# A load moved from SyncE's queue to GpSimd's, a memset moved to VectorE, and another written-out order of 976 steps

## The chip, the cores and the metric

The kernel runs on one core of one Trainium2 chip. The metric is the time of one execution on the device in microseconds, the median of several runs. The engines are called by the profile's short names: PE is TensorE, PEld its weight loads, DVE VectorE, ACT ScalarE, POOL GpSimd and SP SyncE.

## The reference, cut to what matters

Attention without a softmax, through a feature map of degree two, and then a dense layer of width 2048 with a rational activation:

```python
def phi(x):                                       # S1, S2: [8, 32]
    a = np.einsum('rd,bhsd->bhsr', S1, x)
    b = np.einsum('rd,bhsd->bhsr', S2, x)
    return np.einsum('bhsi,bhsj->bhsij', a, b).reshape(*x.shape[:-1], 64)
q_p, k_p = phi(q), phi(k)                         # q, k, v: [4, 4, 1088, 32]
kv, z = np.einsum('bhsf,bhsd->bhfd', k_p, v), np.sum(k_p, axis=2)
x = einsum(q_p, kv) / (einsum(q_p, z) + 1e-06)    # -> [4352, 128]
h = x @ w_in                                      # [128, 2048]
P = a[0] + a[1] * h + a[2] * h**2 + a[3] * h**3
Q = 1.0 + np.abs(b[0]) * np.abs(h) + np.abs(b[1]) * h**2
out = (P / (Q + 1e-06)) @ w_out                   # [2048, 128]
```

All inputs and the output are float32.

## The kernel before

The program is one list of 976 steps. A step is a few instructions of one engine, with the steps that it comes after and the buffers that it uses. `step` (L88) gives the step its place in the program from the tuple `PLACE` (L165), by the number of the step in the order in which the code makes it, and `run` (L99) emits all steps sorted by place. Every engine works through its own instructions in that order. The numbers for cost, rate, slack and `early` that the calls of `step` and `dma` carry are read by nothing in this file; they are the inputs of a planner that wrote `PLACE`. `ON_ACT` (L215) lists the steps that go to ScalarE where either ScalarE or VectorE could do them. `FILLS` (L219) says ahead of which places TensorE gets matmuls on the zero block `idle` that compute nothing; one more is put ahead of all.

Instructions that are not steps are emitted where the code stands, ahead of all steps: GpSimd's memsets of `idle` (L317), of `ones`, the identity, the masks and the constant parts of `v_sb`, `kT` and `kvz` (L318 to L336).

The stages, as far as they are touched:

- S1 and S2 (8x32 each) are loaded into the two halves of `s_raw` by SyncE, k of batch 0 ("k0", 544 KB) by ScalarE's queue, q of batch 0 in two parts and v of batch 0 in two halves by SyncE (L290 to L296), then w_in in two halves, w_out in two halves and k of batch 1 (L303 to L314). A load that finds its DMA semaphore taken waits on the queue for the earlier load that holds it.
- `mk_rep` (L351, DVE) repeats `s_raw` into `s_rep`, `mk_st` (L348, PE) transposes it, `mk_s12` and `mk_sab` (L354, L359, DVE) multiply it with masks into `S12`, the weights of the keys' sketches, and `SAB`, those of the queries'.
- `keys` (L407): VectorE transposes k in blocks of 32 into `kT` (L415, L417), TensorE makes the sketches (L435), ScalarE copies one half of them (L440), VectorE multiplies the halves to features (L443), TensorE adds up features times values (L454), and ScalarE keeps the result in `kvz` (L471).
- `queries` (L487): a transpose of q (L496), sketches (L518 or L546), features (L530, L533, or, through a round trip to DRAM of two puts and three gets, L554), the product with `kvz` (L586), the quotient (L595 to L602), a transpose on TensorE (L608) and the copy into `xT` by ScalarE (L615).
- `w_part` (L385): ten pieces of w_out go to bfloat16, five versions of two halves, `y` 0 to 4; versions 0, 1, 3 and 4 are multiplied by a coefficient (L391, L395), version 2 is a plain copy (L393, L397). Each piece goes to ScalarE or VectorE by `ON_ACT`.
- `unit` (L672): some blocks of 128 hidden channels by up to 512 tokens, 3072 columns in most units, 256 to 2048 in the first and the last ones. TensorE computes h (L688), ScalarE evacuates it (L692), VectorE takes the absolute value (L703), `any_w` (L706: L708 on VectorE, L710 on ScalarE) and L713 form Q, ScalarE inverts it by logarithm and exponential (L716, L719), VectorE forms the powers times the inverse (L728 to L749), and TensorE multiplies by w_out (L784). When a tile of tokens is done VectorE transposes it (L796) and it is written out in pieces (L808).

Of the kernel before, what the change touches and what calls it, by code (L numbers as in the profile page):

```python
# [20 lines left out]
def kernel(  # L21
# [103 lines left out]
    def d_four(n, ptr):  # L125
# [88 lines left out]
    )  # L214
    ON_ACT = (  # L215
        24, 26, 28, 29, 31, 32, 328, 351, 379, 454, 478, 502, 535, 612, 636, 669, 688, 693, 744, 878, 889,
        914, 932, 946, 951, 953, 960,
    )
    FILLS = {5: 15, 14: 4, 66: 5, 70: 1}  # L219
    NW = 5 if '4' in MODES else 3  # L220


    TC = 512
# [32 lines left out]
    def flat(x, b):  # L256
        return x[b].rearrange("h (g j) d -> (h g) (j d)", g=32)
# [605 lines left out]
```

## Time and profile before

| | |
|---|---|
| median of 3 runs | 266.96 us (266.92 to 267.07) |
| the profiled execution | 267.34 us |
| its span, first to last instruction | 265.5 us |
| mean granted TensorE clock | 0.996 |
| DVE busy / ACT busy / PE busy | 252.7 / 248.4 / 257.2 us |
| last instruction of VectorE | 261.75 us, 0.45 long |

The span is what the rows of the profile add up to; the profiled execution is 1.84 us longer than its span. A busy PE is not PE at its peak: matmuls are pipelined, and their ends are modelled. Where an instruction starts before the one ahead of it on its engine has ended, the two overlap in the pipeline, so that distances from start to start say more than durations.

### The profile page before, as it was taken

What the parts mean: (1) busy time and instruction counts of PE and PEld (TensorE: products, weight loads), DVE (VectorE), ACT (ScalarE), POOL (GpSimd) and SP (SyncE); (2) the same over time, 40 slices, a digit from 0 to 9 for tenths busy, and PEclk for the clock granted to TensorE, in tenths of its full rate; (3) what the DMA queues carried; (4) which work ended last, traced back from release to release, by engine and by line L of the source; (5) the groups of instructions that cost most, each with busy time, mean ns of one, the idle gap of its engine ahead of it and who ended that gap; (6) DMA issues with size and microseconds to landing.
All of it is one profiled execution on the core that took longest, in us unless ns stands there. A gap on an engine that the chain in (4) does not pass through costs nothing.

```text
span 265.5 us, 4239 instructions
## 1 busy us (share of the span) xinstructions
PE 257.2 (97%) x1663; PEld 140.4 (53%) x1663; DVE 252.7 (95%) x293; ACT 248.4 (94%) x209; POOL 2.7 (1%) x25
## 2 busy tenths in 40 slices
PE   7999999999999999999999999999999999999994
PEld 5767645644544464344445555444444476565682
DVE  3989899999999999999999999999999999999994
ACT  2499999999999999999999999999999999999991
POOL 4000000000000000000000000000000000000000
PEclk9999999999999999999999999999999999999998
DMA  7948344620556503035001522200002002010032
GB/s 202 331 151 223 121 127 118 159 61 0 145 131 168 164 2 108 13 79 131 28 6 44 150 65 46 41 0 0 0 10 32 0 0 40 4 29 11 0 52 40
DMA packets 29063, 20.13 MB, mean 76 GB/s; under 512 B 19316, under 2 KB 24948, under 8 KB 29044
## 3 DMA queue, kind: packets, MB, share of 16 engines
q1 hardware_dynamic: 28352, 19.24, 28.8%
q10 hardware_dynamic: 692, 0.62, 0.8%
q8 instruction: 13, 0.21, 0.4%
q14 instruction: 6, 0.05, 0.1%
HBM read 16.65 MB, written 3.21 MB: 75 GB/s over the span
## 4 chain that ended last, share of the span: by engine, by line
PE 35%; ACT 29%; DVE 21%; issue 8%; DMA 4%; SPq 1%; DVEq 0%; ACTq 0%
PE h_ps L688 21%; ACT t L692 7%; ACT ln L716 7%; ACT t L719 7%; PE out_ps L784 6%; ACT t L725 5%; DVE t L713 4%; DVE t L728 4%; DVE t L731 3%; DMA kq<-in_q_dram 3%; DVE t L749 2%; PE att_ps L586 2%; DVE t L703 2%; PE att_ps L546 2%; DVE t L708 2%
## 5 line engine op out<-in xcount | busy, mean ns | idle before, releaser
L688 PE MATMUL h_ps<-xT,w_in_sb 128*128 128x512 f32 (+1 forms) x320 | 128.0, 535 | 0.8 <-ACT xT L615 0.6
L784 PE MATMUL out_ps<-t,w_out 128*128 128x512 bf16 (+1 forms) x498 | 101.7, 346 | 0.6 <-DVE t L728 0.5
L688 PEld LDWEIGHTS h_ps<-xT,w_in_sb 128*128 128x128 f32 x320 | 58.6, 190 | 45.2 <-issue 33.8
L784 PEld LDWEIGHTS <-w_out 128*128 128x128 bf16 x498 | 47.4, 98 | 51.9 <-issue 21.1
L692 ACT CAST t<-h_ps 128x1024 bf16<-128x1024 f32 (+1 forms) x69 | 68.5, 1025 | 0.9 <-PE h_ps L688 0.9
L716 ACT ACTIVATE ln<-t 128x3072 f32<-128x3072 bf16 (+4 forms) x29 | 64.7, 2230 | 0.3 <-DVE t L713 0.2
L719 ACT ACTIVATE t<-ln 128x3072 bf16<-128x3072 f32 (+4 forms) x29 | 64.7, 2232 | 0.1
L713 DVE TENSOR_TENSOR t<-t,t 128x3072 bf16<-128x3072 bf16 (+4 forms) x29 | 40.4, 1392 | 0.6 <-ACT t L710 0.6
L728 DVE TENSOR_TENSOR t<-t,t 128x3072 bf16<-128x3072 bf16 (+4 forms) x29 | 40.4, 1394 | 0.0
L731 DVE TENSOR_TENSOR t<-t,t 128x3072 bf16<-128x3072 bf16 (+3 forms) x23 | 32.6, 1423 | 0.1
L725 ACT ACTIVATE t<-t,a_sb 128x3072 bf16<-128x3072 bf16 (+2 forms) x12 | 32.0, 2665 | 0.0
L703 DVE TENSOR_SCALAR t<-t 128x3072 uint16<-128x3072 uint16 (+4 forms) x29 | 22.5, 776 | 0.3 <-ACT t L692 0.2
L734 DVE TENSOR_TENSOR t<-t,t 128x3072 bf16<-128x3072 bf16 (+1 forms) x13 | 21.6, 1660 | 0.0
L708 DVE TENSOR_SCALAR t<-t,b_abs 128x3072 bf16<-128x3072 bf16 (+2 forms) x22 | 21.5, 975 | 0.1
L586 PEld LDWEIGHTS att_ps<-kvz,a_all 128*64 128x64 f32 x288 | 9.6, 137 | 6.8 <-issue 2.2
L586 PE MATMUL att_ps<-kvz,a_all 128*64 128x66 f32 x288 | 11.5, 226 | 0.6 <-DVE a_all L530 0.4
L749 DVE TENSOR_TENSOR t<-t,t 128x1024 bf16<-128x1024 bf16 (+3 forms) x10 | 11.2, 1124 | 0.1
L710 ACT ACTIVATE t<-t,b_abs 128x1024 bf16<-128x1024 bf16 (+4 forms) x7 | 11.3, 1611 | 0.0
L554 DVE TENSOR_TENSOR a_all<-a_all,b_all 128x768 f32<-128x768 f32 (+2 forms) x11 | 9.6, 869 | 0.0
L443 DVE TENSOR_TENSOR k_p<-att_ps,b_sk 128x768 f32<-128x768 f32 x9 | 8.4, 949 | 0.8 <-ACT b_sk L440 0.6
L454 PEld LDWEIGHTS att_ps<-v_sb,k_p 128*64 128x64 f32 x216 | 6.7, 138 | 2.3 <-issue 1.3
L746 DVE TENSOR_TENSOR t<-t,t 128x3072 bf16<-128x3072 bf16 (+3 forms) x6 | 7.7, 1276 | 0.0
(74 smaller groups left out, 143.8 us busy)
## 6 DMA issues: line engine op xcount, KB each, us to landing
a_all<-sk_d SPq DMA_DIRECT2D x6, 384.0 KB, 3.9
b_all<-sk_d SPq DMA_DIRECT2D x12, 192.0 KB
kq<-in_k_dram SPq DMA_DIRECT2D x3, 544.0 KB, 7.3
kq<-in_q_dram SPq DMA_DIRECT2D x3, 544.0 KB
a_all<-sk_d SPq DMA_DIRECT2D x4, 320.0 KB
b_all<-sk_d SPq DMA_DIRECT2D x8, 160.0 KB
v_sb<-in_v_dram SPq DMA_DIRECT2D x4, 288.0 KB, 4.9
v_sb<-in_v_dram SPq DMA_DIRECT2D x4, 256.0 KB, 4.3
```

The source lines that it names most:

```text
L586: nc.tensor.matmul(nd.t[x:x + 64, o:o + 2 * KW], lhsT=(av(c)[:, o0 + x:o0 + x + 64] if how == "direct" else q_p.t[:, c * n + o0 + x:c * n ...
L688: nc.tensor.matmul(h.t[:, cols[x] - cols[x0]:cols[x + 1] - cols[x0]], lhsT=w_in_sb[:, f * 128:(f + 1) * 128], rhs=xT[:, xpos(t0):xpos(t0) ...
L692: nc.scalar.copy(out=hh.t[:, cols[x0]:cols[x1]], in_=h.t[:, 0:cols[x1] - cols[x0]])
L703: nc.vector.tensor_scalar(out=u.t[:, :n].bitcast(U16), in0=hh.t[:, :n].bitcast(U16), scalar1=0x7FFF, scalar2=None, op0=AX.bitwise_and)
L708: nc.vector.tensor_scalar(out=w.t[:, :n], in0=u.t[:, :n], scalar1=ab1, scalar2=ab0, op0=AX.mult, op1=AX.add)
L713: nc.vector.tensor_mul(out=y.t[:, :n], in0=w.t[:, :n], in1=u.t[:, :n])
L716: nc.scalar.activation(out=ln.t[:, :n], in_=y.t[:, :n], func=ACT.Ln, bias=1.0 + 1e-6)
L719: nc.scalar.activation(out=r.t[:, :n], in_=ln.t[:, :n], func=ACT.Exp, scale=-1.0)
L725: nc.scalar.activation(out=p.t[:, :n], in_=hh.t[:, :n], func=ACT.Identity, scale=a3, bias=a2)
L728: nc.vector.tensor_mul(out=s.t[:, :n], in0=hh.t[:, :n], in1=r.t[:, :n])
L731: nc.vector.tensor_mul(out=(hh if mode == 3 else p).t[:, :n], in0=hh.t[:, :n], in1=s.t[:, :n])
L784: nc.tensor.matmul(o[0].t[:, :bl[x][1]], lhsT=w_sb[y_][:, bl[x][2], :], rhs=src.t[:, cols[x]:cols[x + 1]], start=(o[1] == 1), stop=(o[1] = ...
```

## The change

S2's load is no longer a step of SyncE. It is issued by GpSimd where the code stands, ahead of GpSimd's constants, and step 1 is kept as an empty step of GpSimd that later steps come after. `idle` is set to zero by VectorE instead of GpSimd. The numbers given to the planner are others, and with them `PLACE`, `ON_ACT` and `FILLS`. No other step computes anything else or in another form.

Sorted from the two tuples, the first steps of some queues are, by the names of the code:

```
SP before:  S1, S2, q0 first part, v0 low, v0 high, q0 rest, w_out 2nd half, w_out 1st half, w_in 1st half, k1, put, w_in 2nd half
SP after:   S1, q0 first part, v0 low, v0 high, w_out 2nd half, q0 rest, k1, w_out 1st half, w_in 1st half, put, put, w_in 2nd half
DVE before: mk_rep, k0 transposes, mk_s12, q0 transpose, mk_sab, mk_sab, features, k0 transposes, features
DVE after:  mk_rep, mk_s12, k0 transposes, mk_sab, mk_sab, q0 transpose, k0 transposes, features, features
```

`ON_ACT`: of w_out's pieces ScalarE had versions 0, 1 and 4 of the first half, 2 of both and 3 of the second; it has now versions 1, 3 and 4 of the first half and 0, 1 and 3 of the second. Step 946, an `any_w` of 768 columns in the last but one unit, goes from ScalarE to VectorE. The fills are 18 instead of 26.

```diff
--- before.py
+++ after.py
@@ -163,60 +163,60 @@
     PERS = (6,)
     N_T = 16
     PLACE = (
-        0, 3, 1, 19, 6, 7, 8, 2, 18, 16, 9, 58, 55, 12, 10, 4, 5, 13, 24, 25, 49, 21, 23, 22, 83, 97, 84,
...
+        0, 1, 2, 18, 3, 4, 8, 11, 12, 27, 14, 73, 24, 25, 9, 5, 6, 7, 15, 16, 52, 13, 22, 21, 105, 47, 82,
...
     )
     ON_ACT = (
-        24, 26, 28, 29, 31, 32, 328, 351, 379, 454, 478, 502, 535, 612, 636, 669, 688, 693, 744, 878, 889,
-        914, 932, 946, 951, 953, 960,
+        25, 26, 27, 30, 31, 32, 328, 351, 379, 454, 478, 502, 535, 612, 636, 669, 688, 693, 744, 878, 889,
+        914, 932, 951, 953, 960,
     )
-    FILLS = {5: 15, 14: 4, 66: 5, 70: 1}
+    FILLS = {6: 12, 13: 3, 71: 1, 80: 1}
     NW = 5 if '4' in MODES else 3
 
 
@@ -288,12 +288,17 @@
         return dma(s_raw[i * R:(i + 1) * R], s_in, rank, 0.001, eng=eng, cost=0.4, slack=S_SLACK[i], behind=behind)
 
     s_l = [load_s(0, -206, SP)]
-    s_l.append(load_s(1, -205.9, SP, behind=s_l[0]))
+    nc.gpsimd.dma_start(out=s_raw[R:2 * R], in_=S2)
+
+    def go():
+        pass
+
+    s_l.append(step(POOL, 0.65, go, -205.9, land=0.003, early=0.75, slack=0.4))
     FIRST = 256
-    k0_l = load_k(0, k0, -207, slack=0.0, rate=304, eng=ACTE)
+    k0_l = load_k(0, k0, -207, slack=0.15, rate=420, eng=ACTE)
     table = step(ACTE, 1.3, lambda: nc.scalar.preload_act_table_set("natural_log_exp_and_others"), -205, behind=k0_l[0])
-    q0_a = dma(lambda: q0.t[:, 0:FIRST], flat(q, 0)[:, 0:FIRST], -203.8, 0.131, (), [q0], rate=250, slack=0.1, behind=s_l[1])
-    v0_l = load_v(0, v0, -203.7, slack=0.25, rates=(180, 200), behind=q0_a)
+    q0_a = dma(lambda: q0.t[:, 0:FIRST], flat(q, 0)[:, 0:FIRST], -203.8, 0.131, (), [q0], rate=350, slack=0.2, behind=s_l[0])
+    v0_l = load_v(0, v0, -203.7, slack=0.4, rates=(340, 205), behind=q0_a)
     ab_in = []
     for c, w, x in ((4, 2, moe_b), (0, 4, moe_a)):
         ab_in.append(dma(ab_row[:, c:c + w], bass.AP(tensor=x.tensor, offset=x.offset, ap=[[w, 1], [1, w]]), -203.6, 0.001,
@@ -302,19 +307,19 @@
 
     def load_w(x, rank):
         c = x * 1024
-        w_l[x] = dma(w_in_sb[:, c:c + 1024], moe_w_in[:, c:c + 1024], rank, 0.524, early=LATER, rate=300, slack=0.4, behind=v0_l[1])
+        w_l[x] = dma(w_in_sb[:, c:c + 1024], moe_w_in[:, c:c + 1024], rank, 0.524, early=LATER, rate=430, slack=0.4, behind=v0_l[1])
 
     load_w(0, -196)
-    q0_b = dma(lambda: q0.t[:, FIRST:S], flat(q, 0)[:, FIRST:S], Q0B_RANK, 0.426, (), [q0], rate=200, slack=0.3, behind=q0_a)
+    q0_b = dma(lambda: q0.t[:, FIRST:S], flat(q, 0)[:, FIRST:S], Q0B_RANK, 0.426, (), [q0], rate=330, slack=0.4, behind=q0_a)
     load_w(1, W1_RANK)
     k1 = Buf("kq")
-    k1_l = load_k(1, k1, K1L_RANK, early=LATER, slack=0.2, behind=v0_l[1], rate=350)
+    k1_l = load_k(1, k1, K1L_RANK, early=LATER, slack=1.3, behind=v0_l[1], rate=390)
     wo_l = [dma(lambda f0=f0: w_raw.t.rearrange("p (f d) -> p f d", d=d_model)[:, f0:f0 + nf // 2],
                 moe_w_out.rearrange("(fo fi) d -> fi fo d", fi=128)[:, f0:f0 + nf // 2], WO_RANK, 0.525, (), [w_raw],
-                early=LATER, rate=310, slack=0.4, behind=v0_l[1]) for f0 in (0, nf // 2)]
+                early=LATER, rate=318, slack=0.4, behind=v0_l[1]) for f0 in (0, nf // 2)]
 
     idle = consts.tile([128, 256], BF, name="idle")
-    nc.gpsimd.memset(idle, 0.0)
+    nc.vector.memset(idle, 0.0)
     nc.gpsimd.memset(ones, 1.0)
 
     def fill(x):
@@ -367,7 +372,7 @@
             nc.gpsimd.tensor_copy(out=S21[:, :, :, :, hp], in_=S12[:, 2 * hp:2 * hp + 2].rearrange("p h s r -> p s h r"))
 
     st = step(DVE, 0.15, mk_rep, -210, after=s_l)
-    st = step(PE, 0.11, mk_st, -202, after=[st], uses=[s_ps], early=2.7)
+    st = step(PE, 0.11, mk_st, -202, after=[st], uses=[s_ps], early=2.0)
     s12 = [step(DVE, 0.15, mk_s12, -200, after=[st], uses=[s_ps])]
     sab = [step(DVE, 0.2, lambda i=i: mk_sab(i), -201.5 + 0.1 * i, after=[st], uses=[s_ps]) for i in range(2)]
     s21 = step(POOL, 0.4, mk_s21, -196, after=s12)
@@ -560,16 +565,16 @@
             put = [dma(lambda j=j: bass.AP(tensor=d.t.tensor, offset=d.t.offset + j * n2,
                                            ap=[[2 * QN, half], [n, 2], [1, n2]]),
                        lambda j=j: c.t[j * 2 * half:(j + 1) * 2 * half, :n2],
-                       rank, n2 * 256e-6, [st], [c, d], rate=260, slack=GAP) for j in range(2)]
+                       rank, n2 * 256e-6, [st], [c, d], rate=200, slack=GAP) for j in range(2)]
             puts[-1] = put[-1]
             get = [dma(lambda: a.t[:, :2 * n],
                        lambda: bass.AP(tensor=d.t.tensor, offset=d.t.offset, ap=[[2 * QN, 2 * R], [0, R], [1, 2 * n]]),
-                       rank, n * 1.024e-3, put, [d, a], rate=230, cost=0.57, slack=GET_SLACK)]
+                       rank, n * 1.024e-3, put, [d, a], rate=230, cost=0.57, slack=GET_SLACK - 0.2)]
             for h2 in range(2):
                 get.append(dma(lambda h2=h2: bb.t[h2 * 64:(h2 + 1) * 64, :2 * n],
                                lambda h2=h2: bass.AP(tensor=d.t.tensor, offset=d.t.offset + (2 + h2) * R * 2 * QN,
                                                      ap=[[0, R], [2 * QN, R], [1, 2 * n]]),
-                               rank, n * 0.512e-3, put, [d, bb], rate=85, cost=0.6, slack=GET_SLACK, behind=get[-1]))
+                               rank, n * 0.512e-3, put, [d, bb], rate=95, cost=0.6, slack=GET_SLACK, behind=get[-1]))
 
             ft = step(DVE, d_one(2 * n), features, rank, after=get, uses=[a, bb])
 
```

(The tuple `PLACE` is cut to its first line.)

94 rows, old and new, of the table PLACE are left out of this document.

## The prediction

> **What bounds the kernel now.** I read the page's busy times first, then the busy times in windows of 10 us, then the waits, then the first microseconds of the timeline and of the chain of waits.
>
> ```profile
> PE 257.2 (97%) x1663; PEld 140.4 (53%) x1663; DVE 252.7 (95%) x293; ACT 248.4 (94%) x209; POOL 2.7 (1%) x25
> ```
>
> ```profile
> 0.00:10.00 10.00, 8.08 (x109) 6.10 (x110) 5.43 (x16) 2.90 (x10) 2.74 (x25) 1.00 0.87 237
> 10.00:20.00 10.00, 9.44 (x111) 6.95 (x107) 8.63 (x24) 8.11 (x14) 0.00 (x0) 1.00 0.70 221
> 20.00:30.00 10.00, 10.00 (x153) 7.83 (x151) 9.45 (x18) 9.43 (x14) 0.00 (x0) 1.00 0.73 209
> 30.00:40.00 10.00, 9.44 (x51) 4.16 (x48) 9.45 (x17) 9.19 (x14) 0.00 (x0) 1.00 0.38 103
> 60.00:70.00 10.00, 10.00 (x52) 4.90 (x52) 10.00 (x12) 10.00 (x9) 0.00 (x0) 1.00 0.06 13
> 250.00:260.00 10.00, 10.00 (x93) 8.91 (x92) 9.86 (x16) 9.78 (x12) 0.00 (x0) 1.00 0.23 34
> ```
>
> The columns of a window are its length and then the busy time of PE, PEld, DVE, ACT and POOL. VectorE (DVE) works 252.7 us, starts at 4.50 and ends at 262.2, so it stands idle for only 257.7 - 252.7 = 5.0 us on the way, half of that before 35 us. ScalarE is almost as full from 15 us on. The time is therefore VectorE's start, plus its work, plus its stalls, plus 3.3 us of the last transposed block's way out. A change of order can only move these terms.
>
> ```profile
> DVE s_rep L352 <- DMA s_raw<-in_S_dram: 4.5, 1, 4.5
> DVE qT L496 <- DMA kq<-in_q_dram: 0.7, 1, 0.7
> ACT kvz L471 <- PE out_ps L454: 1.7, 1, 1.7
> ```
>
> VectorE starts when S1 and S2 lie in `s_raw`, and has one stall on a load, 0.73 us at 29.8. The first row is what the change aims at:
>
> ```profile
> 0.73 0.74 SPq L268 DMA_DIRECT2D s_raw<-in_S_dram  x2
> 0.74 0.38 ACTq L268 DMA_DIRECT2D kq<-in_k_dram  x1
> ...
> 1.10 0.40 PE L321 MATMUL out_ps<-idle 128*128 128x256 bf16 x1 [1.10 <-POOL idle L317]
> ...
> 4.50 0.21 DVE L352 COPY s_rep<-s_raw 16x128 f32<-16x128 f32 x1 [4.50 <-DMA s_raw<-in_S_dram]
> 4.65 0.75 DVE L415 STREAM_TRANSPOSE kT<-kq 128x256 f32<-128x256 f32 x2
> 4.87 0.20 PE L349 MATMUL att_ps<-ident,s_rep 16*128 16x16 f32 x1 [0.44 <-DVE s_rep L352]
> 5.33 0.17 DVE L355 TENSOR_TENSOR S<-att_ps,mask 128x64 f32<-128x64 f32 x1
> 5.44 0.41 DVE L496 STREAM_TRANSPOSE qT<-kq 128x256 f32<-128x256 f32 x1
> 5.79 0.44 DVE L362 TENSOR_TENSOR SAB<-att_ps,mask 128x128 f32<-128x128 f32 x2
> 6.17 0.42 DVE L443 TENSOR_TENSOR k_p<-h_ps,b_sk 128x256 f32<-128x256 f32 x1
> ```
>
> The semaphore records of the same trace say that S1 landed at 2.17, k0 at 4.36 and S2 at 4.41. S1 and S2 are equal (1 KB), S2 was issued 0.46 us later. The packet records tell why it came 2.24 us later: S1's eight packets ran from 1.68 to 1.85, just ahead of k0's first (1.75); each of S2's eight began 6 ns after k0's last packet on its DMA engine (3.28 to 3.64). An engine that has begun k0's eight rows finishes them first.
>
> **The change, part by part.** The sum is made against the profiled execution (267.34 us, span 265.5), which is 0.38 above the median of the runs; differences are put on the median.
>
> *S2 by POOL.* SP loses one issue, so q0's first part and both halves of v0 are issued 0.33 to 0.46 earlier (1.19 to 1.52, and on). That is worth nothing: after k0 the DMA engines are busy without a gap (share 0.88 to 1.17 in every half microsecond to 7 us), q0's packets follow k0's in any case, and v0 (7.6 for its second half) is no earlier for an earlier issue. On POOL the constants lose the zero block (0.25, spacing 0.73 to 0.98) and stand behind the new issue instead. POOL ends at 3.2 now and the identity at 1.7; nothing asks for them before the transpose of `s_rep`. Even 1.3 us more is hidden there. If the cover is gone, mk_st waits on the identity.
>
> The order of VectorE's first steps, sorted from the new places, is s_rep, S12, k0's two transposes, SAB twice, q0's transpose; now it is s_rep, k0's transposes, S12, q0's transpose, SAB twice. So k0's transposes now queue behind S12, which waits for a TensorE transpose of s_rep. With S2 landing at L: s_rep at L + 0.09 (4.41 to 4.50), mk_st 0.37 later (4.50 to 4.87) and 0.20 long, S12 some 0.10 after that, k0's transposes 0.11 behind it (5.33 to 5.44): L + 0.87. The rest to the first features is 0.68 (4.65 to 5.33) + 0.35 + 0.38 = 1.41, so features begin at L + 2.28 against 6.17: **a shift of L - 3.89**. It can't be better than k0's landing allows: 4.36 + 0.09 + 1.41 = 5.86, a gain of 0.31, reached with L at 3.58 or less.
>
> What is L? No row shows a data DMA issued by POOL. Bounds: the lower end is S1's way, 0.73 to 2.17, if POOL's packets reach the engines by 1.7; the upper is 0.73, an issue as long as SP's longest here (0.75) and S2's present way of 3.22, so 4.7, and behind q0's eight packets on an engine (46 ns each, 0.37) 5.1. Between them a threshold decides: S2's own packets at SP's 0.94 us from issue to first packet would come at 1.68, but k0's engines start at 1.75. 0.1 us of slowness puts S2 behind k0. I take the missed case, with k0's last engine done at 3.97 and a receipt of 0.5 to 0.8 as S2 has now: **L = 4.5, shift +0.6**; ends -0.3 and +1.2.
>
> The Trainium skill ("DMA: Bandwidth & Descriptors", Specifications) gives a first byte of about 1 us for GpSimd's software path and 0.6 for SP's; by it S2's packets would come 0.4 after S1's, at an estimated 2.1, behind k0, and the sum would stay as it is. The same page ("Why a DMA increments its semaphore by 16 and not by 1") says that on this path all 16 engines post the completion whatever the shape; no run here shows that yet, and it would tie S2 to k0's slowest engine instead of eight of them.
>
> *Zero block by VectorE, fills 26 to 18.* VectorE is idle until 4.5, so the memset is free; TensorE's fills may begin up to 0.2 earlier. Thirteen fills at 0.209 (3.14 us for 15) end about 3.7 and hide nothing. Price zero, unless the clock warms later for it: the granted clock was full in the first window it was recorded, and the fills at 5.00 ran in 0.15 each. Bounds 0 and +0.5; I take 0.
>
> *The new order.* The load of q for batch 1, issued at 23.20 behind two puts, goes ahead of one of them; at most the stall of 0.73 goes. ScalarE gets two pieces of w_out (1.16 each, L391) into its idle 1.70 before kvz; it needs w_out's half by 9.3, and that half is now loaded before q0's rest. VectorE's stalls from 10 to 35 us are 2.5 in sum. I take **-0.5**; ends -1.2 and +0.6 (a new stall of the size of those that are there). The price of moving k1 and w_out ahead of w_in: w_in's first half landed at 13.47 and one more load of 1.5 us stands ahead of it now, 15.0, while the first hidden matmul runs at 15.85. 0.85 covers it.
>
> *Who does what.* Step 946, any_w on 768 columns, goes from ScalarE (1.02, L710) to VectorE: 0.48 from L708's 0.54 for 1024 and 0.81 for 2048. It lies in the last 12 us, where VectorE is 9.86 of 10 busy, so it counts in full. Of w_out's ten pieces VectorE swaps two scaled ones (0.74 each) for plain copies, which no row of VectorE shows; ScalarE's are 1.05 against 1.16, so I take -0.1 each, ends 0 and -0.3. Net **+0.3**; ends +0.1 and +0.5.
>
> Sum: +0.6 - 0.5 + 0.3 = +0.4, so 266.96 + 0.4 = **267.4**.
>
> **Rivals.** *S2 slips in ahead of k0* (L under 3.6): -0.3 - 0.5 + 0.3 = -0.5, 266.5. For it: S1 did so, and POOL's first memset starts with SP's first issue (0.73). Against: the margin is 0.07 us. This is the other side, and the point is whether POOL's packets are at the engines by 1.7 to 2.0. *POOL's path is slow* (L about 5.5): +1.6 - 0.5 + 0.3 = +1.4, 268.4. For it: nothing in the trace bounds a first issue by POOL; against: POOL has nothing else to do. *The new order loses*: the planner's rates are those of packets (a 4352-byte packet took 168 ns, which is 414 GB/s over 16 engines, and 420 is in the change), while k0 as a whole took 2.2 us for 557 KB, 250 GB/s. A plan that believes in earlier loads puts steps in order ahead of data; with w_in or q0's rest late by one load (1.5, of which 0.85 is covered) that adds 0.7 and the -0.5 doesn't come: +0.6 + 0.7 + 0.3 with S2 behind k0, -0.3 + 0.7 + 0.3 with S2 early, so 268.6 or 267.7; 268.1 between them. *The change does nothing*: S2 about where it is and order neutral gives the shift of +0.5 by the formula, so this is near the forecast.
>
> **Numbers.** Forecast (S2 behind k0) 0.42, S2 early 0.32, POOL slow 0.13, order loses 0.13. A measurement here can tell about 0.2% (0.53 us) from no change. With each case spread by half a microsecond for the order's ends, the forecast's 0.42 splits into 0.19 slower, 0.17 same, 0.06 faster; the early case's 0.32 into 0.21 faster, 0.09 same, 0.02 slower; the two bad ones' 0.26 is slower but for 0.03 same. That makes faster 0.27, same 0.29, slower 0.44. The range takes the early case's better half to the slow case: 266.2 to 268.6.
>
> **What would show it.** Right: s_rep on VectorE at 4.4 to 4.7, then a gap of 0.4 to 0.6 before S12, k0's transposes after 5.2 and the first features near 6.8; `any_w` of 768 columns on VectorE near 253; no stall of 0.7 on q at 30. Early: s_rep before 4, k0's transposes at 4.45. Slow: s_rep after 5. Order: a new wait of over 0.5 on a load between 8 and 35 us. Wrong altogether: VectorE's stalls after 35 us (2.5 now) changing by more than 1 us, since I hold them equal.

## The result: 2.7 us slower, and in the profile TensorE's clock rises 8.6 us later

The changed kernel took 269.72 us (median of four runs, 268.94 to 270.06) against 267.00 for the kernel before, a ratio of 1.0099 with a 95% interval of 1.0084 to 1.0115. The forecast was 267.4 with a range of 266.2 to 268.6. The profiled execution took 269.63, span 267.8, which is 2.29 over the profiled execution of before.

Four views of the kernel after answer to those shown of before. First the page's busy times:

```profile
PE 256.7 (96%) x1637; PEld 141.7 (53%) x1655; DVE 252.7 (94%) x295; ACT 248.1 (93%) x208; POOL 3.1 (1%) x25
```

VectorE's work is the same 252.7 us, of which 0.17 is now the zero block, at 0.84. So the loss lies in its start and its stalls. The busy times in windows of 10 us (length; PE, PEld, DVE, ACT, POOL; clock, DMA share, GB/s) place it:

```profile
0.00:10.00 10.00, 6.72 (x41) 4.77 (x43) 3.78 (x13) 1.84 (x5) 3.11 (x25) 1.00 0.88 237
10.00:20.00 10.00, 9.94 (x154) 7.50 (x153) 7.80 (x23) 7.70 (x16) 0.00 (x0) 1.00 0.66 190
20.00:30.00 10.00, 9.10 (x87) 7.25 (x86) 8.63 (x15) 9.46 (x15) 0.00 (x0) 1.00 0.99 206
30.00:40.00 10.00, 9.93 (x122) 5.78 (x121) 9.92 (x23) 8.74 (x14) 0.00 (x0) 1.00 0.26 67
```

In the first 20 us VectorE does 11.58 us of work where it did 14.06, a deficit of 2.48. In the next 20 it loses another 0.35 (18.55 against 18.90). In the second window TensorE is busier than before (9.94 against 9.44) while VectorE does less. The waits:

```profile
ACT b_sk L445 <- PE h_ps L440: 7.8, 4, 4.9
DVE s_rep L357 <- DMA s_raw<-in_S_dram: 4.9, 1, 4.9
...
DVE k_p L448 <- ACT b_sk L445: 1.8, 2, 1.6
DVE a_all L559 <- DMA b_all<-sk_d: 1.3, 1, 1.3
```

S2 comes late, the features (`k_p`) have a new wait of 1.57 on ScalarE's copy of the sketches, and further on there is a new wait of 1.30 on a load into `b_all`. The timeline shows where the first two come from (lines of the changed kernel are 5 higher from L317 on):

```profile
0.84 0.17 DVE L322 MEMSET idle<- 128x128 uint32 x1 [0.84 <-PEq L852]
1.23 0.64 POOL L291 DMA_DIRECT2D s_raw<-in_S_dram  x1 [0.78 <-POOLq L852]
1.25 2.77 PE L326 MATMUL att_ps<-idle 128*128 128x256 bf16 x12
...
5.88 0.22 DVE L357 COPY s_rep<-s_raw 16x128 f32<-16x128 f32 x1 [4.87 <-DMA s_raw<-in_S_dram]
6.24 0.26 PE L354 MATMUL att_ps<-ident,s_rep 16*128 16x16 f32 x1 [2.22 <-DVE s_rep L357]
6.60 0.23 DVE L360 TENSOR_TENSOR S<-att_ps,mask 128x64 f32<-128x64 f32 x1 [0.51 <-PE att_ps L354]
6.74 0.76 DVE L420 STREAM_TRANSPOSE kT<-kq 128x256 f32<-128x256 f32 x2
...
7.70 1.12 PE L440 MATMUL h_ps<-S,kT 128*64 128x64 f32 x16
8.75 2.08 PE L523 MATMUL att_ps<-qT,SAB 64*128 64x256 f32 x8
8.93 1.25 DVE L448 TENSOR_TENSOR k_p<-h_ps,b_sk 128x256 f32<-128x256 f32 x2
11.74 0.69 DVE L448 TENSOR_TENSOR k_p<-h_ps,b_sk 128x512 f32<-128x512 f32 x1 [1.57 <-ACT b_sk L445]
```

Set TensorE's lines against the same work in the timeline of before:

```profile
1.29 3.14 PE L321 MATMUL att_ps<-idle 128*128 128x256 bf16 x15
...
5.56 0.69 PE L435 MATMUL h_ps<-S,kT 128*64 128x64 f32 x16
...
6.49 1.13 PE L518 MATMUL att_ps<-qT,SAB 64*128 64x256 f32 x8
```

The sketches (16 matmuls) take 1.12 instead of 0.69, the eight behind them 2.08 instead of 1.13. The trace's record of the granted clock says why: in these two executions full speed begins at 4.02 before and at 12.64 after. TensorE's fills now end at 4.02 instead of 4.43, and then it stands idle for 2.22 us instead of 0.44.

In sum, on VectorE: it starts 1.38 later (4.50 to 5.88), stands idle 1.57 longer from there to 35 us (2.54 to 4.11) and 0.65 less after 35 (2.45 to 1.80); less the 0.17 of work now done ahead of the start that is +2.13. Of the 4.11, 0.51 stands before S12, 1.8 before the features and 1.30 before `b_all`. Its end moved by 2.09 (262.20 to 264.29), which agrees to 0.04.

### The profile page after: what moved, and what is told of

It is laid out like the page before. It is cut to its first block, busy times and chain, and to the rows that moved or that the text cites. A ratio compares the mean times of both kernels' runs of the same rounds, so it can differ in the third digit from the quotient of the medians.

```text
span 267.8 us, 4216 instructions
## 1 busy us (share of the span) xinstructions
PE 256.7 (96%) x1637; PEld 141.7 (53%) x1655; DVE 252.7 (94%) x295; ACT 248.1 (93%) x208; POOL 3.1 (1%) x25
## 4 chain that ended last, share of the span: by engine, by line
PE 50%; ACT 34%; issue 7%; DMA 4%; DVE 2%; SPq 1%; DVEq 0%; ACTq 0%; POOLq 0%
PE h_ps L693 22%; PE out_ps L789 19%; ACT ln L721 10%; ACT t L697 9%; ACT t L724 7%; ACT t L730 6%; DMA b_all<-sk_d 3%; PE att_ps L551 2%; DMA s_raw<-in_S_dram 2%; PE att_ps L591 1%; ACT t L715 1%; PE att_ps L459 1%; PE out_ps L459 1%; ACT xT L620 1%; PE att_ps L613 1%
## 5 line engine op out<-in xcount | busy, mean ns | idle before, releaser
L789 PE MATMUL out_ps<-t,w_out 128*128 128x512 bf16 (+1 forms) x480 | 98.3, 345 | 2.2 <-issue 0.9
L697 ACT CAST t<-h_ps 128x1024 bf16<-128x1024 f32 (+2 forms) x69 | 70.1, 1056 | 1.2 <-PE h_ps L693 1.1
L721 ACT ACTIVATE ln<-t 128x3072 f32<-128x3072 bf16 (+4 forms) x29 | 65.4, 2256 | 0.3 <-DVE t L718 0.2
L724 ACT ACTIVATE t<-ln 128x3072 bf16<-128x3072 f32 (+4 forms) x29 | 65.4, 2255 | 0.2
L736 DVE TENSOR_TENSOR t<-t,t 128x3072 bf16<-128x3072 bf16 (+3 forms) x23 | 33.0, 1433 | 0.0
L713 DVE TENSOR_SCALAR t<-t,b_abs 128x3072 bf16<-128x3072 bf16 (+3 forms) x23 | 21.8, 950 | 0.1
L715 ACT ACTIVATE t<-t,b_abs 128x1024 bf16<-128x1024 bf16 (+3 forms) x6 | 10.2, 1702 | 0.0
L445 ACT COPY b_sk<-h_ps 128x32 f32<-128x32 f32 (+2 forms) x4 | 0.8, 205 | 7.8 <-PE h_ps L440 7.8
```

Source lines behind the costliest of these rows:

```text
L697: nc.scalar.copy(out=hh.t[:, cols[x0]:cols[x1]], in_=h.t[:, 0:cols[x1] - cols[x0]])
L713: nc.vector.tensor_scalar(out=w.t[:, :n], in0=u.t[:, :n], scalar1=ab1, scalar2=ab0, op0=AX.mult, op1=AX.add)
L721: nc.scalar.activation(out=ln.t[:, :n], in_=y.t[:, :n], func=ACT.Ln, bias=1.0 + 1e-6)
L724: nc.scalar.activation(out=r.t[:, :n], in_=ln.t[:, :n], func=ACT.Exp, scale=-1.0)
L736: nc.vector.tensor_mul(out=(hh if mode == 3 else p).t[:, :n], in0=hh.t[:, :n], in1=s.t[:, :n])
L789: nc.tensor.matmul(o[0].t[:, :bl[x][1]], lhsT=w_sb[y_][:, bl[x][2], :], rhs=src.t[:, cols[x]:cols[x + 1]], start=(o[1] == 1), stop=(o[1] = ...
```

## The experiments

Two causes of the loss were to be told apart: S2 landing late (**landing**), and the thinner fills with the longer gap behind them (**clock**). The expectations call the two together theory A and the new order as the cause theory B; A' is the clock by fewer fills alone, and A2 says that the clock decides and the order is worth a little. They count the fills with the one that stands ahead of all, so that their 13, 16, 17 and 21 are 12, 15, 16 and 20 in `FILLS`. Clock and landing times are of the one execution that was profiled. Times are medians; the kernel before ran beside each and took 267.01 to 267.16. Executions of one kernel differ by when the clock rises in them, so that some of these kernels scatter over 3 us; counts of runs are given for that reason.

**S2 back on SP, all else of the change kept.**

```diff
-    nc.gpsimd.dma_start(out=s_raw[R:2 * R], in_=S2)
...
+    s_l.append(load_s(1, -205.9, SP, behind=s_l[0]))
```

> The changed kernel with S2's load back on SyncE (second on its queue, as before), all else as changed. Theory A (S2's late landing and, through it, TensorE's cold clock make the loss; the order is neutral): S2 lands near 4.4 us, s_rep runs at 4.5, the first features at 6.7 (0.5 later than before, since S12 stands ahead of k0's transposes), time 267.0 to 267.8, the higher end if the granted clock is full only after 7 us, because 13 fills end at 4.0 and leave a gap of 0.9. Theory B (the new order itself costs it): the time stays over 269.

Measured: 268.48 (10 runs), ratio 1.0045 (1.0027 to 1.0063). S2 landed at 4.28, s_rep began at 4.38, but the clock rose only at 10.04. So S2's way back takes 1.24 off the 2.72, and 1.44 is left against the kernel before beside it, more than was expected. The 1.24 is not the landing alone: the gap behind the fills also shrinks, from 2.22 to 0.73, and the clock rises at 10.04 instead of 12.64. Theory B, which asked for over 269, does not hold.

**The change with 28 fills at place 6 instead of 12.**

```diff
-    FILLS = {6: 12, 13: 3, 71: 1, 80: 1}
+    FILLS = {6: 28, 13: 3, 71: 1, 80: 1}
```

> The changed kernel with 28 instead of 12 fills ahead of the transpose of s_rep; S2 still by GpSimd. Theory A: S2 lands at 5.8 as in the changed kernel, but TensorE has no gap of 2.2 us, the granted clock is full by 4 to 7.5 us instead of 12.6, and the 16 sketches take 0.7 instead of 1.1 us; 0.8 to 1.1 us of the 2.7 come back: 268.6 to 268.9. Theory B, or S2 alone: no change, 269.7.

Measured: 268.9 (10 runs, 266.54 to 269.56), ratio 1.0052 (1.0026 to 1.0078). The clock rose at 7.09, but at the low clock the fills themselves lasted to 7.3 and held the transpose of s_rep up, so that S12 came at 7.59 instead of 6.60. A cure with its own price; it does not measure the clock's part. Two of the ten took 266.54 and 266.84, less than any other execution with S2 by POOL (267.72 at the least). No trace of them is kept, so what came early in them is open, and a late landing may not cost its full price in every execution.

**The kernel before, with S2 by POOL and the zero block by VectorE.** The order and the 16 + 4 fills stay.

```diff
-    s_l.append(load_s(1, -205.9, SP, behind=s_l[0]))
+    nc.gpsimd.dma_start(out=s_raw[R:2 * R], in_=S2)
...
-    nc.gpsimd.memset(idle, 0.0)
+    nc.vector.memset(idle, 0.0)
```

> The kernel before, its order and fills, with S2 issued by GpSimd ahead of its constants and the zero block filled by VectorE: the change without its order. Theory A: S2 lands at 5.5 to 5.9, s_rep at 5.6 to 5.9, VectorE's start moves by 1.1 to 1.4, the gap after 16 fills is 1.5, so 268.1 to 268.5 with a warm clock and up to 269.3 with a cold one. Theory B: 267.0, the order alone is to blame.

Measured: 269.58 (4 runs), ratio 1.0096 (1.0067 to 1.0126). S2 landed at 5.68. That is 2.54 us for a landing 1.27 later (4.41 before): the clock rose at 4.75, fell back at 8.16 and rose again at 11.57. TensorE stood idle for 1.41 between the fills and the transpose of s_rep, where it was 0.44 before, so that here the late S2 costs clock too, and the time lies above the 269.3 that was allowed for that.

**The kernel before with three fills fewer, and nothing else.**

```diff
-    FILLS = {5: 15, 14: 4, 66: 5, 70: 1}
+    FILLS = {5: 12, 14: 4, 66: 5, 70: 1}
```

> The kernel before with 13 instead of 16 fills ahead of the transpose of s_rep, nothing else: the clock's part by itself. The fills end near 3.8 and leave a gap of 1.1 (0.4 before). Theory A': a gap of this size already keeps the granted clock low for some executions, time 267.0 to 268.0 with a spread of over 0.5. Rival: only gaps over 2 us matter, 267.0 and the clock full near 4 us.

Measured: 269.28 (10 runs, nine of them 268.98 to 269.62, one 266.63), ratio 1.0075 (1.0052 to 1.0098). Its timeline:

```profile
1.28 2.77 PE L321 MATMUL att_ps<-idle 128*128 128x256 bf16 x12
4.78 0.26 PE L349 MATMUL att_ps<-ident,s_rep 16*128 16x16 f32 x1 [0.73 <-DVE s_rep L352]
4.97 1.03 PE L321 MATMUL out_ps<-idle 128*128 128x256 bf16 x4
5.93 1.12 PE L435 MATMUL h_ps<-S,kT 128*64 128x64 f32 x16
...
7.51 2.08 PE L518 MATMUL att_ps<-qT,SAB 64*128 64x256 f32 x8
```

S2 is as early as ever (s_rep at 4.42). The fills are 0.37 shorter and the gap behind them 0.29 longer, and full speed begins at 13.01 instead of 4.02. The same sizes as in the changed kernel, 1.12 and 2.08, and 2.24 us on the whole kernel, more than either side expected. The pair of traces alone would not show it, since the moments at which the clock can change lie on a grid that differs from execution to execution (last section). The count does: nine of ten executions take 268.98 or more, and all 25 of the kernel before beside them 266.56 to 267.56. The clock's part is shown by itself.

**S2 on SP and 16 fills.** The first experiment with as many fills ahead of the transpose of s_rep as before (behind it 3, where the kernel before has 4).

```diff
-    FILLS = {6: 12, 13: 3, 71: 1, 80: 1}
+    FILLS = {6: 15, 13: 3, 71: 1, 80: 1}
```

> The changed kernel with S2 by SyncE and 16 fills ahead of the transpose of s_rep, as many as before: the new order with the start of before. Theory A: S2 at 4.4, clock full near 4 us, S12 ahead of k0's transposes costs 0.5, the rest of the order is worth -0.5 to +0.3: 267.0 to 267.8. Theory B: over 268.5.

Measured: 266.66 (10 runs, 265.7 to 269.36), ratio 1.0009 (0.9979 to 1.0038). With both causes undone the loss is gone in six runs of ten (265.7 to 266.85, below what was expected); one took 267.69, and three (268.11 to 269.36) are as slow as the kernels whose clock rises late. In the profiled execution, 266.85, it rose at 5.48.

**S1 loaded into both halves by one load**, so that S2's rows are S1's and nothing waits for S2. S2 is left out. It was meant to give an early landing.

```diff
-    s_l = [load_s(0, -206, SP)]
-    nc.gpsimd.dma_start(out=s_raw[R:2 * R], in_=S2)
+    s_l = [dma(s_raw, bass.AP(tensor=S1.tensor, offset=S1.offset, ap=[[0, 2], [D, R], [1, D]]), -206, 0.001)]
```

> The changed kernel with S1 loaded into both halves of s_raw by one load of SyncE, and no load of S2: this leaves S2 out and so shows the new order with both halves there when its plan wants them. Lands near 2.1 us. Theory A: s_rep before 2.7, S12 before 3.5, k0's transposes as soon as k0 is there (4.4 to 5.0), first features at 5.9 to 6.5; the granted clock depends on the gap after 13 fills, which now is filled by no work until 5 us; time 266.3 to 267.3. Theory B: over 268.5.

Measured: 268.6 (266.45 to 269.49), ratio 1.0044 (1.0018 to 1.007). It did not come early: this load was issued over 0.82 us and landed at 4.39, no earlier than S2 from SP. The clock rose at 9.34, and the kernel tells no more than the first experiment.

**S12 and k0's first transposes exchanged in the order**, on the kernel with S2 on SP and 16 fills, so that the transposes no longer queue behind S12.

```diff
     PLACE = (
-        0, 1, 2, 18, 3, 4, 8, 11, 12, 27, 14, 73, 24, 25, 9, 5, 6, 7, 15, 16, 52, 13, 22, 21, 105, 47, 82,
-        63, 104, 61, 81, 46, 106, 84, 10, 26,
+        0, 1, 2, 18, 3, 4, 8, 11, 12, 27, 14, 73, 24, 25, 9, 5, 6, 10, 15, 16, 52, 13, 22, 21, 105, 47, 82,
+        63, 104, 61, 81, 46, 106, 84, 7, 26,
...
```

> As the kernel with S2 by SyncE and 16 fills in the new order, and k0's first transposes ahead of S12 on VectorE (two places exchanged), as the order of before had them. Theory A (S12's wait in front of k0's transposes costs 0.5): 0.3 to 0.5 us faster than the same kernel without the exchange, 266.6 to 267.3. Rival (something later in the order bounds the start): no difference between the two.

Measured: 266.67 (10 runs), ratio 0.9994 (0.997 to 1.0018), against 266.66 without the exchange. The gain of 0.3 to 0.5 did not come: the 0.51 us that VectorE waits for S12 is worth nothing that can be told in the whole time. Two of the ten runs took 268.8 and 269.36.

**S2 on SP, fills 16 and 5**, against the kernel with S2 on SP and 16 fills.

```diff
-    FILLS = {6: 15, 13: 3, 71: 1, 80: 1}
+    FILLS = {6: 16, 13: 5, 71: 1, 80: 1}
```

> The new order with S2 by SyncE, and 17 fills ahead of the transpose of s_rep and 5 behind it (the kernel before has 16 and 4; the change 13 and 3). Theory A2 (the loss is TensorE's granted clock, which the thinner fills let rise late, and with an early clock the new order is worth about 0.5 to 0.9): all executions near 266.1 to 266.7, none over 267.5, the granted clock full before 7.5 us. Rival (the clock's rise is luck, whatever the fills): some executions at 268.5 to 269.4, as in the same kernel with 16 and 3.

Measured: 267.15 (12 runs, 265.75 to 267.92), ratio 0.9998 (0.9982 to 1.0013): no execution is over 268 any more, but the median is above the 266.1 to 266.7 that was expected, and the new order is worth nothing that can be measured. The fastest of them was profiled:

```profile
1.24 3.62 PE L321 MATMUL att_ps<-idle 128*128 128x256 bf16 x16
4.47 0.21 DVE L352 COPY s_rep<-s_raw 16x128 f32<-16x128 f32 x1 [3.47 <-DMA s_raw<-in_S_dram]
6.87 1.14 PE L518 MATMUL att_ps<-qT,SAB 64*128 64x256 f32 x8
7.52 1.88 DVE L443 TENSOR_TENSOR k_p<-h_ps,b_sk 128x256 f32<-128x256 f32 x3
```

**The change, with fills 20 and 6.** S2 by POOL, but with fills that reach nearly to the transpose of s_rep (a gap of 0.40).

```diff
-    FILLS = {6: 12, 13: 3, 71: 1, 80: 1}
+    FILLS = {6: 20, 13: 6, 71: 1, 80: 1}
```

> The changed kernel, S2 by GpSimd, with 21 fills ahead of the transpose of s_rep (they end near 5.5 us, S2 lands at 5.8) and 6 behind it. Theory A2: in the executions in which the clock rises early the time is 266.5 to 267.2, so that S2's late landing by itself costs 0.4 to 0.7 and the change would have made no difference with a warm clock; others up to 269. Rival (S2's landing is the larger part): nothing under 268.

Measured: 268.5 (4 runs, 267.72 to 269.44), ratio 1.0063 (1.0038 to 1.0087). The clock rose at 6.46, ahead of the sketches:

```profile
1.25 4.47 PE L326 MATMUL att_ps<-idle 128*128 128x256 bf16 x20
5.76 0.21 DVE L357 COPY s_rep<-s_raw 16x128 f32<-16x128 f32 x1 [4.76 <-DMA s_raw<-in_S_dram]
7.43 0.69 PE L440 MATMUL h_ps<-S,kT 128*64 128x64 f32 x16
8.16 1.14 PE L523 MATMUL att_ps<-qT,SAB 64*128 64x256 f32 x8
8.81 1.87 DVE L448 TENSOR_TENSOR k_p<-h_ps,b_sk 128x256 f32<-128x256 f32 x3
```

0.69 and 1.14 again, and no wait among the features: k0's last features begin 6.17 behind s_rep, where the change had 7.80 (13.68 less 5.88). The difference of 1.63 is what the low clock takes there. The median lies above the 266.5 to 267.2 of theory A2; only the fastest run is under the 268 below which the rival allowed none. Against the kernel with fills 16 and 5 everything up to the features is later by the same 1.29 (4.47 to 5.76, 7.52 to 8.81): that is the landing alone. The four medians make a table:

| | S2 by POOL | S2 by SP |
|---|---|---|
| fills 12 + 3 | 269.72 | 268.48 |
| fills that raise the clock early | 268.5 | 267.15 |

By the medians the landing costs 1.24 and 1.35 and the clock 1.22 and 1.33, so about the same with the other cause there or not. No more than that is shown: the runs of one cell scatter over 1.1 to 2.2 us, the two cells by POOL have four runs each, and the two fills of the lower row are not the same (20 + 6 and 16 + 5).

**All 16 rows of s_raw from one load of rows of w_in** (S1 and S2 are left out), fills 6 and 13, so that the rows come early.

```diff
-    s_l = [load_s(0, -206, SP)]
-    nc.gpsimd.dma_start(out=s_raw[R:2 * R], in_=S2)
+    s_l = [dma(s_raw, moe_w_in[0:2 * R, 0:D], -206, 0.001)]
```

> The new order with all 16 rows of s_raw from one load of SyncE of 16 other rows (of w_in): S1 and S2 are left out. 7 fills ahead of the transpose of s_rep, 14 behind it. One load on 16 DMA engines should land ahead of k0, near 2.1, S12 be done by 3.5 and k0's transposes start when k0 lands (4.4). If an early S2 is what the plan of the change lives on: first features at 5.9 to 6.2, 265.5 to 266.2. Rival (k0, v0 and the rest of the loads bound the start): no faster than the order with S2 by SyncE, 266.1 to 266.7.

Measured: 266.61 (10 runs), ratio 0.9985 (0.9968 to 1.0001). The load landed at 2.34, s_rep ran at 2.36 and S12 at 3.51, but k0's transposes began at 4.76, when k0 had landed at 4.73. With an S that is 2 us early the median is 0.54 lower (267.15 to 266.61), which the scatter of the two (265.84 to 267.89 here) does not tell from nothing; in the trace k0 sets the start, as the rival had it. The fills are other ones, too (13 behind the transpose, where the expectation says 14).

**S2 loaded again in mid-kernel into scratch tiles, by POOL and by ScalarE's queue**, twice each, once among other transfers and once in quiet.

```diff
+                if i in (9, 13) and x0 == 0:
+                    nc.gpsimd.tensor_copy(out=scr[i], in_=hh.t[0:R, 0:D])
+                    nc.gpsimd.dma_start(out=scr[i], in_=S2)
+                if i in (10, 14) and x0 == 0:
+                    nc.scalar.dma_start(out=scr[i], in_=S2)
```

> The kernel before with four more loads of S2 into a scratch tile in the middle of the work, two issued by GpSimd and two by ScalarE, when few other transfers run: the path of a 1 KB load by each by itself. If GpSimd's way is slower by itself: 0.4 to 1.0 us more from issue to landing than ScalarE's. Rival (it is only the crowd of k0's and q0's packets that made S2 late): both land within 0.3 us of each other, some 1.5 to 2 us from the issue's start.

One execution, 266.74. The quiet pair in the timeline:

```profile
128.84 0.72 POOL L696 DMA_DIRECT2D scr<-in_S_dram  x1 [0.30 <-POOL scr L695]
...
130.17 0.28 ACTq L698 DMA_DIRECT2D scr<-in_S_dram  x1
```

From the start of the issue POOL's first packet came after 1.34 and its data had landed after 1.83; ScalarE's after 0.88 and 1.25. So POOL's way is 0.58 longer by itself, of which 0.44 is the longer issue (0.72 against 0.28). Among other transfers the two took 5.28 and 4.01.

**The exchanged order with S2 on SP and fills 15 and 4**, against the kernel of the exchange.

```diff
-    FILLS = {6: 15, 13: 3, 71: 1, 80: 1}
+    FILLS = {6: 15, 13: 4, 71: 1, 80: 1}
```

> The version that the runs point to: the new order with S2 by SyncE, k0's first transposes ahead of S12 on VectorE, and 16 fills ahead of the transpose of s_rep and 4 behind it, as many as the kernel before has. Theory A2 (order worth a little, the clock decides): no execution over 268, median 266.4 to 266.8, 0.1 to 0.25% faster than the kernel before. Rival (the order is worth nothing once the fills are the same): 267.0 to 267.2, no difference that can be told.

Measured: 266.47 (12 runs, 265.78 to 269.47), ratio 0.9986 (0.9962 to 1.001). It has the lowest median, yet the interval holds 1: two of the twelve runs are at 268.93 and 269.47, and the profile of the first of these has the clock rise at 10.06, so the expectation of none over 268 missed. No version here is shown to beat the kernel before.

## Why the prediction was wrong

The direction was right and the size was not. **The step that failed is the price of the fills**: "Price zero, unless the clock warms later for it", with bounds of 0 and +0.5. By the medians it is 1.2 to 1.3 in the changed kernel, and 2.24 when it is the only change. The condition was named, and a row read as if it spoke against it: full clock in the first window recorded (the record begins with the rise itself, at 4.02), and fills at 5.00 in 0.15 each. That row told that the clock was up with sixteen fills; it told nothing of thirteen. The note that the fills "hide nothing" looked for cover of time, where their work is to keep TensorE busy.

**L, the landing of S2, was mis-sized**: 4.5 taken, 5.1 as the upper end, 5.85 measured. Its mechanism held: S2's packets ran from 3.85 to 4.01, behind k0, and for six of the eight a packet of q0 ends within 9 ns before and none of k0, so these came behind q0 as well, as only the upper end had it. (In the kernel before the packets' ends put seven of S2's eight 2 to 3 ns behind one of k0, where the prediction has 6.) Three things went with it. POOL's issue began at 1.23, not at 0.73 as in both ends of L, and took 0.64. The load's completions then came one by one from 4.44 to 5.85, sixteen of them, the last 1.07 after the last completion packet (4.78), where 0.5 to 0.8 had been taken. And k0 itself landed at 4.96 instead of 4.36. All four profiles with S2 by POOL are alike in this: fourteen of the sixteen completions by 4.98, the last at 5.68 to 5.94, and k0 at 4.89 to 5.07, against 4.36 to 4.57 in the eight with S2 on SP. So k0's last completion comes late with it; why, no run shows. The Trainium skill ("DMA: Bandwidth & Descriptors", Why a DMA increments its semaphore by 16 and not by 1) was quoted as saying that on POOL's path all 16 engines post whatever the shape; the trace agrees, with sixteen semaphore events for a load of eight rows. By the measured L the sum would have been +2.0 - 0.5 + 0.3 = +1.8, so 268.8, still 0.9 short.

**The chain behind S2 held in part.** The transpose of s_rep came 0.36 after it (0.37 forecast), k0's transposes at L + 0.89 (0.87). The first features came at L + 3.08, not L + 2.28: the new order puts k0's second pair of transposes ahead of them. VectorE works through that stretch with no gap but the 0.51 before S12, in the kernel with S2 on SP too (features 3.05 after s_rep, against 1.67 before), so the delay of the first features measures nothing; the formula was right for the start and wrong for what it called its end.

**The new order** was put at -0.5 and any_w with w_out at +0.3, -0.2 together. With both causes undone that is +0.0 (fills 16 + 5) or -0.35 (15 + 3), neither told from no change. Single steps came as forecast: any_w on 768 columns takes VectorE 0.48 at 250.63, and the stall of 0.73 on q is gone. The wait of 1.30 on `b_all` up to 27.54, whose last load is issued at 20.20 behind another put, is the sign that the prediction set for the rival "the new order loses": a new wait of over 0.5 on a load between 8 and 35 us. Nine of the ten profiles of the new order have it (1.16 to 2.67), the fastest execution with fills 16 and 5 alone has not, and none of the four of the old order has it. The rival's loss of 0.7 did not come: with both causes undone the order is even. In that fastest execution VectorE's stalls up to 35 us are 1.52, against 2.54 before; what the order would be worth without this wait in all executions is open. VectorE's stalls after 35 us fell by 0.65, inside the bound of 1 that would have spoken against holding them equal.

**The sum, with measured terms**: landing 1.24 to 1.35, clock 1.22 to 1.33, order 0 to -0.35, which is 2.1 to 2.7 against the 2.72 found. That is no test of the terms: landing and clock are differences of the same four medians, and along either way through the table they add up to 2.57 by themselves. The rival "POOL's path is slow" (268.4 at L of 5.5) had the landing nearly right and the clock as little as the forecast did.

**What stays open** is what makes the clock rise. In the kernel before with three fills fewer, TensorE's row shows no idle time from 4.78 on, and yet the clock rose only at 13.01. In the profile of the exchanged order with fills 15 and 4 TensorE was busy for 1.00 of the step from 3.24 to 6.65, with fills for 0.72 of it, and the clock stayed low at its end. Small matmuls may count for less than fills over the whole array; these traces speak for it, but no run varies that alone.

## What to carry to other kernels

Work that computes nothing can still hold a price: before removing filler matmuls ahead of a TensorE phase, look up when the clock rose in the trace of before, and cost the change as the phase behind it at the low clock (here the sketches and features, 1.63 us up to k0's last features). Count executions, too: one trace can show the rise of a lucky one. Where a load is moved to another queue, price its issue, the first packet and the last completion each from a row of that queue; where none exists, put the upper end past the slowest neighbour and let it count. A delay of the first consumer costs only the idle time it makes on the bounding engine.

## What the runs showed of the hardware

- **The clock changes on a grid of 3.41 us that the kernel's start does not set.** In the kernel before with S2 by POOL it changed at 4.75, 8.16 and 11.57, in steps of 3.41, and the long records of full clock in the fourteen profiles last 252.59, 256.00 or 259.41 us, which is 74, 75 or 76 such steps. Counted back from the rise, the first step after the kernel's start lies anywhere from 0.26 to 3.24. The Trainium skill ("TensorE: Matmul & The Clock Gate", Part 1: The HAM clock gate) speaks of a free-running window of about 3.4 us, which agrees, and advises not to fit to a count of cold matmuls, since the ramp is under 1% of a typical kernel; here three fills moved 2.24 of 267 us, 0.8%, and four times the 0.53 that the prediction took a measurement to tell apart.
- **An early rise went with a step of the grid that fills nearly filled.** This is an estimate from the timelines and the clock records, since the ends of matmuls are modelled. In the eight profiles with an early rise, fills took these shares of the step that ended with it: 0.85 (rise at 4.02), 0.96 (4.37), 0.97 (4.75), 0.95 (5.21), 0.96 (5.48), 0.82 (5.89), 0.83 (6.46) and 1.00 (7.09). Of the steps ahead of a rise after which the clock stayed low none had more than 0.78 of fills; in that one TensorE was busy for 0.99. Twelve fills and a first one run from 1.05 or 1.10 to 4.05 at the latest, which is at most 0.88 of a step, and so nearly fill one only where the grid lies well for them, which fits nine late executions of ten. It is read from fourteen executions and not tested.
- **The clock column of a window is no witness for its first microseconds.** The window from 0 to 10 us shows 1.00 before and after, though the record starts at 12.64 in the second. The durations of equal matmuls show it: 0.69 and 1.12 for sixteen sketches.
- **Nearly equal kernels, and executions of one kernel, can rise early or late.** Of the kernels with S2 on SP and 15 or 16 fills at place 6, profiled executions of 265.75 and 266.85 us have the rise at 5.21 and 5.48, those of 268.8 and 268.93 at 9.65 and 10.06; the first steps of the grid lie at 1.80 and 2.07 in the early ones, at 2.82 and 3.24 in the late ones. One kernel's ten runs go from 265.7 to 269.36. A profile of one execution may show the rarer case.
- **A small load by POOL starts late and takes longer**: the issue began 0.49 after SP's first and ScalarE's first (1.23 against 0.74), and in quiet the way was 1.83 against 1.25.
